# Part of a sliding convolution moved from TensorE to VectorE and GpSimd

## The chip, the cores and the metric

The kernel runs on one core of a Trainium2 chip. The metric is the time of one execution on the device, in microseconds; before the change the median of three runs is 519.91 us (519.69 to 520.58).

TensorE (PE in the profile) multiplies matrices from SBUF into PSUM, which has eight banks here used as four pairs. VectorE (DVE), ScalarE (ACT) and GpSimd (POOL) work element by element; GpSimd's instructions here work in SBUF only. SyncE (SP) issues DMAs. Each engine runs its own instructions in order and waits on semaphores for the others.

## The reference

x is 8 x 3904 x 192; eight heads of 24 channels each have seven taps.

```python
w = softmax(weight, axis=-1)                      # 8 x 7
x_pad = concatenate([zeros((B, 6, D)), x], axis=1)
conv[b, s, h, g] = sum_k w[h, k] * x_pad[b, s + k, h, g]
t = conv.reshape(31232, 192)
out = (((t @ w1) * (t @ w2)) @ w3) @ w_out        # 1024 wide inside, 192 at the end
```

## The kernel before, in words

**Streams and rounds.** The 31,232 tokens are two streams of 15,616 (NS = 2), the first and the last four batches, which are computed side by side. A round is 512 tokens of both streams; there are 31 (the last of 256), in eight groups of four (the last group of three). The product w3 @ w_out is computed once (W_sb), so a round is two products: first_product makes ab = (t w1) * (t w2), TensorE at L381, ScalarE's cast at L389, VectorE's multiply at L400; second_product makes out = ab @ W_sb, TensorE at L434, ScalarE's copy at L439, and an output DMA at L446. In a group the first products of its four rounds come first (the first stage), then the eight second products, two to a round (the second stage).

**Convolution.** TensorE convolves in windows. A window is 64 tokens on 64 partitions, of which 58 come out; a banded 64 x 64 matrix with the taps of a head (Aband) multiplies it. A batch has 68 windows, a stream 272. conv (L274 to L312) takes a block of windows, half of them to the lower and half to the upper 64 output partitions, and convolves nh heads of it: for each head four matmuls (L290) of n x 24 columns, n being half of the block's windows. The result is cast to bf16 into convo (L311). SIZES lists the blocks: six small ones for the start, then six of 36. load_x fetches a block, with a cast to bf16, by DMAs on GpSimd's queue (L119).

**From convolution to product.** The product wants channels on the partitions, the convolution leaves tokens there. So store (L316 on) writes convo to a DRAM tensor, rows, by DMAs on SP's queue (L334), and transposes(R) (L363) reads round R back into xT by three transposing DMAs, also on SP's queue. xT is a ring of four rounds: round R + 4 takes the place of round R, so its transposes wait until round R's first product has read it. send issues the transposes of all rounds that are wholly in rows.

**Order around the change.** The order of each engine's instructions is that of the code. In the loop over groups p (at the end of the kernel), block 6 + p is loaded while the group's first two rounds run (a one-element copy on GpSimd, pace, L592, holds the loads back until the round's product is done) and convolved between the second products: heads 0 to 2 after the second of them, 3 to 5 after the fourth, 6 and 7 after the eighth, and then stored. VectorE casts it, ScalarE one head of it. The convolution is so some six rounds ahead of the products. The output DMAs are issued by SP, in group 0 by GpSimd. Block 5 belongs to group 0 as well. The eight W products (w3_product, L469) precede group 0's second stage.

PSUM pairs are handed out by banks() from a list and given back by drained(); the order of this list decides which earlier reader a matmul waits for.

Of the kernel before, what the change touches and what calls it, by code (L numbers as in the profile page):

```python
# [8 lines left out]
FP32 = mybir.dt.float32  # L9
# [7 lines left out]
def kernel(  # L17
# [34 lines left out]
    FIRST = [sum(SIZES[:b]) for b in range(NB)]  # L52
    PROLOGUE_BLOCKS = 6
    EARLY = SIZES[0] * ST
    MAXN = max(SIZES) // 2

    def tok(i):
        return (i // WB) * S + (i % WB) * ST
# [199 lines left out]
        return p, Aband[:, g, e], bps[:, :, 0:Q]  # L258


    xT = [const.tile([128, RING + Q], BF16, name=f"xT{k}", tag=f"xT{k}") for k in range(NP)]

    convo_of = {}
# [10 lines left out]
    def conv(b, h0, nh, evict=None):  # L274
        n = SIZES[b] // 2
        if h0 == 0:
            convo_of[b] = work.tile([128, n, NP, NS, Q], BF16, tag="convo", bufs=2, name="convo")
        convo = convo_of[b]
        p, cps = banks()
        wd = nh * G  # L280
# [174 lines left out]
    w3T = const.tile([128, JT, DFF], BF16)  # L455
    w3rows = dram.tile([DFF, DFF], BF16, name="w3rows")

    def load_w3(j):
# [100 lines left out]
    P(out=pace, in_=w3T[0:1, JT - 3, DFF - 2:DFF])  # L559
    load_x(5)  # L560
    load_x(6)
    first_product(3)
# [5 lines left out]
    def conv_heads(b, heads, last, f=(nc.vector.tensor_copy,), nh=1):  # L568
        for j, h in enumerate(heads[::nh]):
            conv(b, h, nh, (f[j % len(f)],))  # L570
        if heads[-1] == H - 1:
            first = min(need(sent[0]), FIRST[b] + SIZES[b])
            store(b, last=first)
            send(last)
            store(b, first)
            send(last)

    slots = (range(0, 3), range(3, 6), range(6, H))
    zero(5)
    for jt in range(JT):  # L580
        w3_product(jt)

    groups = [list(range(R, min(R + GROUP, NR))) for R in range(0, NR, GROUP)]
    assert groups[-1][-1] == NR - 1
    for p, rounds in enumerate(groups):
        b = PROLOGUE_BLOCKS + p
        order = rounds[-1:] + rounds[:-1] if rounds[-1] == NR - 1 else rounds
        for j, R in enumerate(order if p else ()):
            first_product(R, behind_conv=j == 0 and b <= NB)
            send(R + GROUP)  # L590
            if j < 2 and b < NB:
                P(out=pace, in_=abT_of[R][0:1, JT - 1, 1, 0:2])  # L592
                load_x(b, (j,))
        if b < NB:
            zero(b)
        ahead = rounds[-1] + GROUP
        at = {1: [(b, slots[0], ahead)], 3: [(b, slots[1], ahead)],
              7: [(b, slots[2], ahead, (V, A))]}
        if p == 0:
            at = {0: [(5, range(0, 6), ahead, (V, A), 2)], 1: [(5, range(6, H), ahead, (V,), 2)],  # L600
                  4: at[1], 5: at[3], 7: at[7]}
# [4 lines left out]
    assert sent[0] == NR  # L606


# [28 lines left out]
```

## Time and profile before

| | us |
|---|---|
| median of 3 runs | 519.91 (519.69 to 520.58) |
| the profiled execution | 520.47 |
| its span, first to last instruction | 518.8 |
| TensorE matmuls busy | 512.4 |
| VectorE busy | 352.8 |
| ScalarE busy | 328.7 |
| GpSimd busy | 58.5 |
| first products, matmuls (L381, all forms) | 319.9 |
| second products, matmuls (L434) | 164.9 |
| convolution, matmuls (L290) | 16.7 |

A row of a group reads: line, engine, operation, output<-input, partitions x elements and type, count | busy us, mean ns of one | idle time of the engine just before, and who ended it. A row of the chain in order of time reads: start, length, what. DMA lines with sixteen engines' share count a packet's time as the profiler saw it.

### The profile page before, as it was taken

The page shows a single profiled execution, that of the slowest core. Times are in us where ns is not written, and L with a number is a line of the kernel's source. Part 1 is how long each engine was busy: PE and PEld are TensorE (multiplying, and loading weights), DVE is VectorE, ACT ScalarE, POOL GpSimd, SP SyncE. Part 2 cuts the span into 40 slices and gives each one's busy share as a digit, 9 for nine tenths or more (in the row PEclk, how much of TensorE's full clock was granted, in tenths as well). Part 3 has the DMA queues.
Part 4 walks back from the last instruction along what each step waited for, and adds up shares of the span by engine and source line. Part 5 has one row for each costly group of instructions (what it writes and reads, how often), then busy time and mean ns, then how long its engine had stood idle before and what let it go on. Part 6 is the DMA issues. An engine that isn't in the chain of part 4 may idle for free.

```text
span 518.8 us, 13029 instructions
## 1 busy us (share of the span) xinstructions
PE 512.4 (99%) x5576; PEld 338.7 (65%) x5576; DVE 352.8 (68%) x334; ACT 328.7 (63%) x415; POOL 58.5 (11%) x98
## 2 busy tenths in 40 slices
PE   8999999999999999999999999999999999999997
PEld 4455797445884558845588455884558845599567
DVE  6778625999439994399943999439994399921980
ACT  6887634777347773477734777347773477734762
POOL 8501522110001200011000120001200000000000
PEclk9999999999999999999999999999999999999999
DMA  9979997599246992469924699246992465124004
GB/s 117 162 145 133 156 201 202 137 178 119 93 134 134 151 121 92 135 117 142 143 92 136 141 141 122 93 136 147 133 121 93 136 146 96 37 92 153 1 3 152
DMA packets 133576, 64.61 MB, mean 125 GB/s; under 512 B 90460, under 2 KB 132798, under 8 KB 133454
## 3 DMA queue, kind: packets, MB, share of 16 engines
q1 hardware_dynamic: 94476, 44.06, 41.7%
q0 software_dynamic: 38896, 19.62, 29.1%
q8 instruction: 43, 0.70, 0.6%
q14 instruction: 15, 0.12, 0.1%
q10 hardware_dynamic: 146, 0.10, 0.1%
HBM read 33.25 MB, written 36.52 MB: 134 GB/s over the span
## 4 chain that ended last, share of the span: by engine, by line
PE 95%; DMA 2%; ACT 2%; DVE 1%; issue 0%; ACTq 0%; DVEq 0%
PE pairs L381 58%; PE pairs L434 31%; PE pairs L290 3%; DMA xT<-rows 2%; DVE abT L400 1%; PE pairs L469 1%; ACT asb L389 1%; PE pairs L206 1%; PE pairs L343 1%; PE pairs L256 0%; ACT wd L186 0%; ACT convo L311 0%; DVE convo L478 0%; ACT xT L355 0%; PE pairs L509 0%
## 5 line engine op out<-in xcount | busy, mean ns | idle before, releaser
L400 DVE TENSOR_TENSOR abT<-asb,pairs 128x1024 bf16<-128x1024 bf16 (+1 forms) x245 | 297.9, 1217 | 52.6 <-ACT asb L389 36.6
L381 PE MATMUL pairs<-xT,wd 64*128 64x512 bf16 (+3 forms) x3000 | 319.9, 371 | 1.1 <-DMA xT<-rows 0.5
L389 ACT CAST asb<-pairs 128x1024 bf16<-128x1024 f32 (+1 forms) x245 | 247.2, 1009 | 66.2 <-PE pairs L381 65.9
L381 PEld LDWEIGHTS <-wd 64*128 64x128 bf16 x3000 | 161.0, 94 | 154.8 <-issue 3.7
L434 PEld LDWEIGHTS <-abT 128*128 128x128 bf16 x1952 | 160.0, 98 | 7.5 <-issue 7.5
L434 PE MATMUL pairs<-W_sb,abT 128*128 128x192 bf16 x1952 | 164.9, 246 | 0.0
L439 ACT COPY osb<-pairs 128x384 f32<-128x384 f32 x122 | 58.3, 478 | 113.8 <-PE pairs L434 113.8
L311 DVE CAST convo<-pairs 128x864 bf16<-128x864 f32 (+5 forms) x58 | 46.4, 854 | 95.8 <-PE pairs L290 74.9
L119 POOL DMA_DIRECT2D xb<-in_x_dram x42 | 32.2, 784 | 3.7 <-PE pairs L381 3.7
L592 POOL COPY pace<-abT 1x2 bf16<-1x2 bf16 x10 | 1.8, 176 | 253.5 <-DVE abT L400 253.5
L290 PE MATMUL pairs<-xb,Aband 64*64 64x432 bf16 (+5 forms) x384 | 16.7, 284 | 0.1
L311 ACT CAST convo<-pairs 128x864 bf16<-128x864 f32 (+4 forms) x20 | 11.8, 626 | 0.4
L290 PEld LDWEIGHTS <-Aband 64*64 64x64 bf16 x384 | 6.9, 106 | 6.8 <-issue 5.7
L446 POOL DMA_DIRECT2D out_dram<-osb x8 | 6.1, 761 | 16.7 <-ACT osb L439 14.1
L439 DVE COPY osb<-pairs 128x192 f32<-128x192 f32 x1 | 0.4, 358 | 11.1 <-PE pairs L434 11.1
L469 PEld LDWEIGHTS <-w3T 128*128 128x128 bf16 x64 | 5.2, 98 | 0.4 <-issue 0.4
L469 PE MATMUL pairs<-wo_b,w3T 128*128 128x192 bf16 x64 | 5.5, 246 | 0.0
L190 POOL COPY wd<-wd 64x768 bf16<-64x768 bf16 x6 | 4.8, 840 | 0.4 <-DMA wd<-in_moe_w_dram 0.4
L206 PE MATMUL pairs<-zeros 128*128 128x512 bf16 x8 | 3.8, 627 | 1.1 <-DVE ones L152 1.1
L343 PE MATMUL pairs<-ident,convo 128*128 128x128 bf16 x48 | 3.9, 219 | 0.7 <-DVE convo L478 0.6
L343 PEld LDWEIGHTS <-convo 128*128 128x128 bf16 x48 | 2.9, 97 | 2.5 <-issue 1.5
L471 ACT CAST W_sb<-pairs 128x192 bf16<-128x192 f32 x8 | 2.6, 320 | 2.8 <-PE pairs L469 2.8
(52 smaller groups left out, 38.8 us busy)
## 6 DMA issues: line engine op xcount, KB each, us to landing
out_dram<-osb SPq DMA_DIRECT2D x52, 384.0 KB
xb<-in_x_dram POOLq DMA_DIRECT2D x16, 432.0 KB, 11.6
rows<-convo SPq DMA_DIRECT2D x5, 648.0 KB
out_dram<-osb POOLq DMA_DIRECT2D x8, 384.0 KB, 3.9
w3rows<-in_moe_w_dram POOLq DMA_DIRECT2D x2, 1024.0 KB, 11.5
xb<-in_x_dram POOLq DMA_DIRECT2D x8, 240.0 KB, 5.5
xT<-rows SPq DMA_TRANSPOSE x81
rows<-convo SPq DMA_DIRECT2D x3, 432.0 KB
```

The source lines that it names most:

```text
L119: nc.gpsimd.dma_start(out=xb[Q * r:Q * r + Q, w:w + m, :], in_=x_spans(r, i, m))
L206: nc.tensor.matmul(t[:, j % 2, :], zeros, zeros[:, 0:1].to_broadcast([128, CH]), start=True, stop=True)
L290: nc.tensor.matmul(view(slice(Q * c, Q * c + Q), r)[:, :, j * G:(j + 1) * G], band_of(h, r), xb[Q * r:Q * r + Q, w0:w0 + n, h * G:(h + 1) ...
L311: f[e % len(f)](out=dst, in_=part)
L343: nc.tensor.transpose(out=tps[:, w, :], in_=convo[:, w, k].rearrange("p r g -> p (r g)"), identity=ident)
L381: nc.tensor.matmul(p[:, r, e * n:e * n + n], wd[i][rs, k, ft * 128:(ft + 1) * 128], xT[k][rs, r0 + c0:r0 + c1], start=(k == 0), stop=(k == ...
L389: nc.scalar.copy(out=asb, in_=pa)
L400: nc.vector.tensor_tensor(out=dst, in0=asb, in1=pb, op=ALU.mult)
L434: nc.tensor.matmul(ops[:, (g - g0) * D:(g - g0) * D + D], ab[:, jt, r, g * 128:(g + 1) * 128], W_sb[:, jt, :], start=(jt == 0), stop=(jt = ...
L439: f(out=osb[:, g0:g0 + per, :].rearrange("p g d -> p (g d)"), in_=ops[:, 0:per * D])
L446: queue.dma_start(out=out[t0:t0 + ng * 128, :].rearrange("(g p) d -> p g d", p=128), in_=osb)
L469: nc.tensor.matmul(wps[:, 0, 0:D], w3T[:, gt, jt * 128:(jt + 1) * 128], wo_b[:, gt, :], start=(gt == 0), stop=(gt == JT - 1))
```

## The change

Blocks. After the start-up blocks 0 to 4 the grid of windows goes on in blocks of 20, 20, 14, 20 and 18 (5 to 9), which end inside round 14. Rounds 16 and 17, 20 and 21, 24 and 25 are each convolved by TensorE as a block of 18 windows of their own (ALONE), in groups 2 to 4. The last 24 windows are the last block, in group 5. Rounds 14 and 15, 18 and 19, 22 and 23, 26 and 27 (SHARED) are not on TensorE: in groups p = 2 to 5 VectorE and GpSimd convolve them.

Shared rounds. load_shared brings 1024 tokens of both streams as 128 partitions of 8 consecutive tokens and the 6 before them, so that a tap is a shift along the free dimension. Where a batch begins inside (7808 in the tile of p = 2, 11712 in that of p = 4), the six rows before it are overwritten with zeros by another DMA, which waits for the load. shared_head convolves one head. GpSimd takes heads 0 to 3: seven multiplications into fp32 tiles, the taps broadcast, and additions, the last of them in two or four pieces into y; all four heads stand at the group's head in its order, and behind them the loads for the next group. VectorE takes heads 4 to 7: ScalarE writes the first tap's product into a PSUM bank, five fused multiply-adds follow there, and the last tap goes in two or four pieces into y. Heads 4 and 5 come before the second stage, 6 after its second and 7 after its fourth product. They use one PSUM pair, held from before the stage to its end. store_shared writes y into rows after the stage, with the transposes of both rounds behind it.

The rest. conv_heads takes two or three heads at a time; ScalarE casts the lone blocks and most of the last one. Taps are computed a second time on all partitions (wv), between the first and the second W product. w3T shares its buffers with the shared tiles. From group 2 on, the transposes of the next group's first two rounds follow the first two first products, with no pace copies.

```diff
-    SIZES = [6, 4, 8, 10, 8, 20] + [36] * 6
-    assert sum(SIZES) == NWIN
+    SIZES = [6, 4, 8, 10, 8, 20, 20, 14, 20, 18]
+    SHARED = {p: ((p + 2) * GROUP - 2, (p + 2) * GROUP) for p in range(2, 6)}
+    ALONE = {p: (p + 2) * GROUP for p in range(2, 5)}
+    CA = 2 * CH
...
+    NA = 2 * (-(-CA // (2 * ST)))
+    GRID = len(SIZES)
+    SIZES += [NA] * len(ALONE) + [24]
...
+    def load_shared(v):
+        t0, W = share(v)
+        xv = work.tile([128, W + PAD, NS, D], BF16, tag="xw", bufs=2, name="xv")
+        for r in range(NS):
+            nc.gpsimd.dma_start(out=xv[:, :, r, :], in_=bass.AP(
+                tensor=x.tensor, offset=(r * TS + t0 - PAD) * D,
+                ap=[[W * D, 128], [D, W + PAD], [1, D]]))
...
+    def shared_head(v, h, f):
...
+        on_vector = f is nc.vector
+        if on_vector:
+            acc = held[0][1][:, h % 2, 0:W * NS * G]
+        else:
+            acc = work.tile([128, W * NS * G], FP32, tag="acc", bufs=2, name="acc")
...
+        if on_vector:
+            nc.scalar.activation(out=flat, in_=xs(PAD), func=ACT.Copy, scale=tap(PAD))
+            for k in range(PAD - 1, 0, -1):
+                f.scalar_tensor_tensor(out=flat, in0=xs(k), scalar=tap(k), in1=flat,
+                                       op0=ALU.mult, op1=ALU.add)
+            for dst, r, cs in parts:
+                f.scalar_tensor_tensor(
+                    out=dst, in0=xv[:, 0:W, r, h * G + cs.start:h * G + cs.stop],
+                    scalar=tap(0), in1=by_row[:, :, r, cs], op0=ALU.mult, op1=ALU.add)
+            return
+        wide = lambda k: tap(k).unsqueeze(2).to_broadcast([128, W * NS, G])
+        f.tensor_tensor(out=flat, in0=xs(PAD), in1=wide(PAD), op=ALU.mult)
+        for k in range(PAD - 1, -1, -1):
+            term = work.tile([128, W * NS * G], FP32, tag="term", bufs=2, name="term")
+            f.tensor_tensor(out=term.rearrange("p (m g) -> p m g", g=G), in0=xs(k),
+                            in1=wide(k), op=ALU.mult)
+            if k:
+                f.tensor_tensor(out=acc, in0=acc, in1=term, op=ALU.add)
+        term = term.rearrange("p (s r g) -> p s r g", r=NS, g=G)
+        for dst, r, cs in parts:
+            f.tensor_tensor(out=dst, in0=by_row[:, :, r, cs], in1=term[:, :, r, cs], op=ALU.add)
...
-    slots = (range(0, 3), range(3, 6), range(6, H))
...
+    at = {
+        (0, 0): [(conv_heads, 5, SHORT, (V, A))],
+        (0, 1): [(conv_heads, 5, LONG), (put_rows, 5, 2 * GROUP - 1), (load_x, 7)],
+        (0, 4): [(conv_heads, 6, SHORT, (V, A))],
+        (0, 5): [(conv_heads, 6, LONG), (put_rows, 6, 2 * GROUP - 1)],
+        (0, 6): [(conv_heads, 7, range(H), (A, V), 3)],
+        (0, 7): [(put_rows, 7, 2 * GROUP - 1)],
+        (1, 1): [(conv_heads, 8, SHORT)],
+        (1, 3): [(conv_heads, 8, LONG), (store, 8),
+                 (conv_heads, 9, range(0, 4))],
+        (1, 7): [(conv_heads, 9, range(4, H), (V, A)), (put_rows, 9, 3 * GROUP - 1)],
+        (5, 0): [(conv_heads, NB - 1, range(0, 2), (A,), 1)],
...
+    for p in ALONE:
+        at[p, 0] = [(conv_heads, GRID - 2 + p, range(0, 4), (A,))]
+        at[p, 3] = [(conv_heads, GRID - 2 + p, range(4, H), (A,)), (store_alone, p)]
+    for p in SHARED:
+        for i, h in ((-1, 4), (-1, 5), (1, 6), (3, 7)):
+            at.setdefault((p, i), []).append((shared_head, p, h, nc.vector))
+    behind = {
+        (1, 0): [(load_x, 8)], (1, 1): [(load_x, 9)], (1, 3): [(load_shared, 2)],
+        (4, 1): [(load_x, NB - 1)]}
...
     for p, rounds in enumerate(groups):
-        b = PROLOGUE_BLOCKS + p
         order = rounds[-1:] + rounds[:-1] if rounds[-1] == NR - 1 else rounds
+        if p in SHARED:
+            for h in range(0, 4):
+                shared_head(p, h, nc.gpsimd)
+            if p + 1 in ALONE:
+                load_alone(p + 1)
+            if p + 1 in SHARED:
+                load_shared(p + 1)
         for j, R in enumerate(order if p else ()):
-            first_product(R, behind_conv=j == 0 and b <= NB)
-            send(R + GROUP)
-            if j < 2 and b < NB:
+            first_product(R, behind_conv=j == 0 and p in (2, 6))
+            if p == 1:
+                send(R + GROUP)
+            elif R + GROUP < NR and (j < 2 or p > 5):
+                transposes(R + GROUP)
+            if p == 1 and j != 2:
                 P(out=pace, in_=abT_of[R][0:1, JT - 1, 1, 0:2])
-                load_x(b, (j,))
...
+            run(behind.get((p, j), ()))
+            if p == 1 and j == 3:
+                load_alone(2)
+        if p in SHARED:
+            held.append(banks())
+            run(at.get((p, -1), ()))
         for i, (R, r) in enumerate((R, r) for R in rounds for r in range(NS)):
             second_product(R, r, R == NR - 1 and r == 1, nc.sync if p else nc.gpsimd)
-            for c in at.get(i, ()) if b < NB else ():
-                conv_heads(*c)
+            run(at.get((p, i), ()))
+        if p in SHARED:
+            drained(held.pop()[0])
+            store_shared(p)
+            for R in range(*SHARED[p]):
+                transposes(R)
```

More of the change, by code (lines that the diff above doesn't have):

```diff
@@ L261, with store_shared @@
+    def store_shared(v):
+        t0, W = share(v)
+        y = shared.pop(v)[1]
+        nc.sync.dma_start(
+            out=rows[t0:t0 + 128 * W, :].rearrange("(p s) c -> p (s c)", s=W),
+            in_=y.rearrange("p s k r q -> p (s k r q)"))
     xT = [const.tile([128, RING + Q], BF16, name=f"xT{k}", tag=f"xT{k}") for k in range(NP)]
@@ L561 @@
     load_x(6)
+    wv = const.tile([128, H, K], FP32)
+    top = const.tile([128, H], FP32)
+    nc.sync.dma_start(out=wv, in_=bass.AP(
+        tensor=weight.tensor, offset=0, ap=[[0, 128], [K, H], [1, K]]))
     first_product(3)
@@ new lines, with run @@
+    for p in ALONE:
+        at[p, 0] = [(conv_heads, GRID - 2 + p, range(0, 4), (A,))]
[6 more added lines that the diff above has]
+        (4, 1): [(load_x, NB - 1)]}
+    def run(calls):
+        for f, *a in calls:
+            f(*a)
@@ L597 @@
[L597 to L601, printed above, removed]
+        if p in SHARED:
[5 more added lines that the diff above has]
+                load_shared(p + 1)
```

96 lines of the change are left out of this document (77 added, 19 removed).

## The prediction

> **What bounds the kernel now.** I read the page first: engine totals, the forty slices, the chain that ended last.
>
> ```profile
> span 518.8 us, 13029 instructions
> PE 512.4 (99%) x5576; PEld 338.7 (65%) x5576; DVE 352.8 (68%) x334; ACT 328.7 (63%) x415; POOL 58.5 (11%) x98
> ...
> DMA  9979997599246992469924699246992465124004
> ...
> PE 95%; DMA 2%; ACT 2%; DVE 1%; issue 0%; ACTq 0%; DVEq 0%
> PE pairs L381 58%; PE pairs L434 31%; PE pairs L290 3%; DMA xT<-rows 2%; DVE abT L400 1%; PE pairs L469 1%; ACT asb L389 1%; PE pairs L206 1%; PE pairs L343 1%; PE pairs L256 0%; ACT wd L186 0%; ACT convo L311 0%; DVE convo L478 0%; ACT xT L355 0%; PE pairs L509 0%
> ```
>
> TensorE is the chain almost everywhere, so an edit pays only in TensorE time. The convolution, L290, has 3% of it. Then the chain in order of time, which prices a group:
>
> ```profile
> 58.94 5.39 PE pairs L469 x64
> ...
> 66.97 0.74 PE pairs L290 x24
> 67.71 2.75 PE pairs L434 x32
> 70.45 0.33 PE pairs L290 x8
> ...
> 88.78 23.17 PE pairs L381 x213
> 111.94 8.86 DMA xT<-rows
> 120.80 0.04 issue
> 120.84 10.11 PE pairs L381 x92
> ...
> 154.22 41.55 PE pairs L381 x384
> 195.77 5.39 PE pairs L434 x64
> 201.16 0.67 PE pairs L290 x12
> 201.83 5.39 PE pairs L434 x64
> 207.21 0.67 PE pairs L290 x12
> 207.88 10.67 PE pairs L434 x128
> 218.55 0.49 PE pairs L290 x8
> 219.04 41.55 PE pairs L381 x384
> ```
>
> A group is 64.82 us (219.04 - 154.22): 41.55 of first products, about 21.4 of second products, and 0.67 + 0.67 + 0.49 = 1.83 for a convolution block of 36 windows. There is no gap. The other engines in group 0's second products and in group 2's two stages (sums by windows; columns PE, PEld, DVE, ACT, POOL, then clock, DMA share, GB/s):
>
> ```profile
> 58.90:88.80 29.90, 29.90 (x388) 27.58 (x388) 11.32 (x15) 11.68 (x27) 7.20 (x11) 1.00 1.07 204
> ...
> 154.20:195.80 41.60, 41.60 (x390) 20.60 (x387) 38.47 (x32) 32.84 (x34) 5.35 (x10) 1.00 0.99 130
> 195.80:219.00 23.20, 23.20 (x290) 21.56 (x291) 7.67 (x11) 7.98 (x17) 0.00 (x0) 1.00 0.36 120
> ```
>
> In the first stage (second row) VectorE is within 8% of TensorE and the DMA engines are full (share 0.99). In the second (third row), VectorE and ScalarE are two thirds idle, the DMA share is 0.36, and GpSimd does nothing. The clock is 1.00 throughout.
>
> **What TensorE loses and keeps.** Convolved windows fall from 272 to 206 (128 + 3 x 18 + 24), because eight rounds leave the grid. A matmul's columns are 12 times the block's windows. Two block sizes have chain rows: 20 windows (240 columns) took 0.74 + 0.33 = 1.07 us, 36 windows (432 columns) 1.83. A line through both gives 0.12 + 0.00396 per column, hence 0.79 for 14 windows (168), 0.98 for 18 (216) and 1.26 for 24 (288). From block 5 on, before: 1.07 + 6 x 1.83 = 12.05. After: three blocks of 20 (3.21), one of 14 (0.79), one of 18 (0.98), three lone blocks of 18 (2.93) and one of 24 (1.26): 9.17. **Saved: 2.9 us.** Bounds: the 216-column block lies between half of 1.83 and the 1.07 of 240 columns, so 0.92 to 1.07, which over four such blocks is -0.2 to +0.4.
>
> Smaller terms. The wait at 111.94, the transposes of round 7, cost group 1 about 0.6 us (130.95 - 88.78 = 42.17 against 41.55). Block 6 is now stored after the sixth second product instead of the eighth, 6 us earlier, but into full DMA engines: 0 to 0.6, I take 0.3 saved. The pair of PSUM banks held for VectorE leaves three pairs in the second stage. A second product's last eviction is 0.48 us (row below) and the narrow convolution slots between two products last 0.3 to 0.6, so the product behind them finds its pair free or about 0.15 us late; some four slots in group 5 and the odd one elsewhere: 0 to 1.0, I take 0.5 lost. The second set of tap weights is some ten tiny instructions on VectorE and ScalarE beside the eight W products (5.4 us of TensorE): 0 to 0.3, taken as nothing.
>
> **VectorE and ScalarE in the second stage.** A tap is a two-input instruction, one input from SBUF and one from PSUM, the operand kinds of L400:
>
> ```profile
> L400 DVE TENSOR_TENSOR abT<-asb,pairs 128x1024 bf16<-128x1024 bf16 x242 | 295.3, 1221 | 51.6 <-ACT asb L389 35.6
> L311 DVE CAST convo<-pairs 128x864 bf16<-128x864 f32 x30 | 30.6, 1054 | 87.8 <-PE pairs L290 67.0 <-DMA out_dram<-osb 20.8
> ...
> L400 DVE TENSOR_TENSOR abT<-asb,pairs 128x696 bf16<-128x696 bf16 x2 | 1.8, 880 | 1.0 <-ACT asb L389 1.0
> ...
> 126.20 6.40 DVE L400 TENSOR_TENSOR abT<-asb,pairs 128x1024 bf16<-128x1024 bf16 x5
> ```
>
> The slope is (1221 - 880) / 328 = 1.04 ns per element, so a tap of 384 elements is 0.56 us, the closing ones of 192, 128 and 64 are 0.36, 0.29 and 0.22. Four heads: 20 x 0.56 + 6 x 0.36 + 2 x 0.29 + 2 x 0.22 = 14.4 us. They replace some 7 us of casts and start when the last product of the stage is done, 1.65 us behind TensorE (in group 1, 126.20 + 6.40 against 130.95): heads 4 and 5 end near 9, 6 near 13, 7 near 16 of 22.4 us. The cover is six microseconds. If a fused multiply-add cost twice the two-input row, 28.8 us would run some 8 past the stage, of which the first stage's slack takes back 2.5 (41.6 - 38.47 less the tail): about 5 us a group, 20 in four.
>
> ```profile
> L439 ACT COPY osb<-pairs 128x384 f32<-128x384 f32 x121 | 58.0, 479 | 112.9 <-PE pairs L434 112.9
> L311 ACT CAST convo<-pairs 128x864 bf16<-128x864 f32 x6 | 5.3, 879 | 0.3
> ...
> L478 ACT CAST convo<-pairs 128x384 bf16<-128x384 f32 x2 | 0.9, 474 | 0.0
> ```
>
> ScalarE gets four first taps (four times 0.47) and the casts of the lone block (four times 0.9 to 1.0): 8.0 + 1.9 + 3.8 = 13.7 of 22.4. A first tap into a bank half waits for the head two before it; head 6's is issued near 6 us and head 4 ends near 5, so the evictions queued behind it on ScalarE aren't held.
>
> **GpSimd, the term that decides.** Per group it gets four heads: 48 instructions of 384 elements and 10 closing ones that make up four times 384, 58 instructions and 19,968 elements. No row shows two inputs there; the nearest:
>
> ```profile
> L119 POOL DMA_DIRECT2D xb<-in_x_dram x42 | 32.2, 784 | 3.7 <-PE pairs L381 3.7
> ...
> L190 POOL COPY wd<-wd 64x768 bf16<-64x768 bf16 x6 | 4.8, 840 | 0.4 <-DMA wd<-in_moe_w_dram 0.4
> ...
> L592 POOL COPY pace<-abT 1x2 bf16<-1x2 bf16 x10 | 1.8, 176 | 253.5 <-DVE abT L400 253.5
> ```
>
> One stream costs (840 - 176) / 766 = 0.87 ns per element over a fixed 0.18. With the copy's rate for two inputs, the floor, a group is 17.3 + 10.2 = 27.5 us; with three times it (two reads and a write in turn), 62.1. I take twice, one stream per input, because the copy is the only streaming row: 34.6 + 10.2 = **44.8 us**.
>
> [...]
>
> What is it late for? Its queue runs heads(p), then the loads of the lone block (four issues of 0.78) and the shared tile of p+1, then heads(p+1), which wait for that tile. The DMA view of 154 to 220 us prices a load (packets, MB, share of 16 engines):
>
> ```profile
> q0 software_dynamic: 4704, 1.77, 24.6%
> ```
>
> 24.6% of 66 us over 4704 packets is 3.45 ns a packet of 384 bytes. The shared tile is 128 x 14 x 2 = 3584 packets, 12.4 us; a lone block 2304, 7.9. The first tile is issued when round 7's product is done, at 132.6 (126.20 + 6.40). The stores of 384 KB that a page row shows to landing bound the new store:
>
> ```profile
> out_dram<-osb POOLq DMA_DIRECT2D x8, 384.0 KB, 3.9
> ```
>
> The tile lands near 146; the zeros of a batch start inside it wait for that (some 3 us), then four issues: heads(2) from 152. Gaps between head sets: 21 us, 24 (with such zeros again) and, with no lone block, 13: 58 together. Groups 2 to 4 are now 41.55 + 21.44 + 0.98 = 64.0 us each, so groups 3, 4, 5 and 6 start at 218.4, 282.3, 346.3 and 410.5 (group 5 keeps 1.26 of convolution). The two shared rounds come third and fourth: first needed 20.8 us into the next group, and before that their store (384 KB landed in 3.9 us; this one is twice that, say 4) and the transposes (8.86 in the chain): GpSimd must end by 8 us into the next group, 418.3 for the last. 152 + 4H + 58 = 418.3 gives **H = 52.1 us**; at 44.8 it ends 29 us early, and beyond 52.1 each microsecond per group is four at the end. At 62.1 that is 40 us. SP issues this store and six transposes behind the last output store and waits there for GpSimd; queued behind are the next group's transposes and outputs, needed a group later.
>
> **Does GpSimd slow VectorE?** In the start-up it copied weights while VectorE multiplied:
>
> ```profile
> 13.76 1.60 POOL L190 COPY wd<-wd 64x768 bf16<-64x768 bf16 x2
> ...
> 14.56 3.75 DVE L400 TENSOR_TENSOR abT<-asb,pairs 128x1024 bf16<-128x1024 bf16 x3 [0.59 <-ACT asb L389]
> ...
> L400 DVE TENSOR_TENSOR abT<-asb,pairs x33: 840/1221/1222, 10.8 to 59.4; 128x1024 bf16<-128x1024 bf16 x30, 128x696 bf16<-128x696 bf16 x2, 128x656 bf16<-128x656 bf16 x1
> ```
>
> The longest multiply there is 1222 ns against a median of 1221, beside copies or not. I cost it at nothing; two-input GpSimd work isn't in the trace, so the other end is a wait of half a GpSimd instruction (0.42 us) for each of the 32 multiplies in a stage, 13.4 less the slack of 2.5, some 11 us in each of four stages.
>
> **The sum.** The profiled execution took 520.47 us (518.8 of it span): -2.9 -0.3 +0.5 = 517.8. The median of the three runs, 519.91, lies 0.56 below that execution, so the forecast for the median is **517.2 us**. About 0.2% (1 us) is what a measurement of this kernel tells from no change.
>
> **Rivals.**
> 1. GpSimd is late (slower). Place: the first product of the third round of groups 3 to 6. It decides from 52.1 us per set of heads. For it: the price rests on a one-input row, and the loads stand between the sets. Against: 7 us of margin in each set. Halfway from the threshold to the upper bound, H = 57, it costs 20 us: 537; all of it spans 519 to 557.
> 2. VectorE becomes the bound, by port waits (4 x 11: 561) or by dear fused taps (537). The multiply rows speak against both.
> 3. The gain is given back: waits of some 3 us, 520. Block 7 is loaded once block 5 has left its buffers (70.78) and convolved after seven second products and two blocks (64.33 + 7 x 2.7 + 2 x 1.07 = 85.4); Its 14 x 128 packets take 6.2 us at 3.45 ns, but the DMA engines are over-full there (share 1.07), and the load waits behind others.
> 4. It does what it says but short matmuls cost more than the line: 518.5; this lies in the forecast's own range.
>
> **Chances.** Forecast with the fourth 0.54 (516.0 to 518.9); GpSimd late 0.29; VectorE 0.09; given back 0.08. Faster by over 0.2%: 0.54 and a hair of the third, 0.55. Within 0.2%: most of the third, 0.07. Slower: 0.38. The range runs from 515.6 (bounds of the savings added, no bank waits) up to 537, where half of the first rival and part of the second are left out.
>
> **What would show it.** Right: L290 in groups 2 to 4 adds to about 1.0 us in the chain, which stays without a transpose wait before the third round; GpSimd's two-input instructions near 0.85 us, a set under 52; L400 still at 1221. Wrong: a DMA or GpSimd piece in the chain some 21 us into groups 3 to 6, growing from group to group (rival 1); multiplies longer than 1222, or taps above 0.6 us (rival 2).

## The result and the profile after

The changed kernel takes 534.82 us (median of 4 runs, 531.53 to 538.59) against 519.88 (519.69 to 520.58): a ratio of 1.027, 95% interval 1.022 to 1.032. It is slower; the forecast was 517.2 with a range up to 537 and a chance of 0.38 for slower. The profiled execution took 534.05 us.

The page of the changed kernel, engine totals, slices and GpSimd's and VectorE's new groups:

```profile
span 532.3 us, 13534 instructions
...
PE 515.2 (97%) x5640; PEld 344.8 (65%) x5640; DVE 385.5 (72%) x423; ACT 348.2 (65%) x459; POOL 254.1 (48%) x333
...
PEclk9999999799999999999999999999899999999999
...
L328 POOL TENSOR_TENSOR acc<-acc,term 128x384 f32<-128x384 f32 x80 | 79.7, 997 | 6.3
L325 POOL TENSOR_TENSOR term<-xv,wv 128x384 f32<-128x384 bf16 x96 | 79.3, 826 | 3.3 <-DMA xv<-zeros 3.3
L314 DVE SCALAR_TENSOR_TENSOR pairs<-xv,wv,pairs 128x384 f32<-128x384 bf16 x80 | 49.8, 622 | 4.2 <-ACT pairs L312 1.9
```

L381 is now L486 (first products), L434 L539 (second), L290 L395 (convolution), L400 L505 (VectorE's multiply), L363 L468 (transposes). TensorE's granted clock dips in two slices (digits 7 and 8). Both lie where it waits for transposes or just behind (who waited for whom: us in total, times, longest):

```profile
PE pairs L486 <- DMA xT<-rows: 9.5, 5, 3.4
PE pairs L539 <- DVE abT L505: 1.7, 4, 0.4
```

And the chain in order of time, where it departs from the one of before:

```profile
82.46 1.90 PE pairs L539 x22
84.36 10.93 DMA xT<-rows
...
95.34 43.83 PE pairs L486 x380
...
162.53 39.62 PE pairs L486 x366
...
202.18 1.02 ACT asb L494
...
203.22 1.23 DVE abT L505
...
204.50 2.80 PE pairs L539 x32
207.30 0.49 PE pairs L395 x16
...
226.98 39.62 PE pairs L486 x366
...
355.87 15.11 PE pairs L486 x139
370.98 10.12 DMA xT<-rows
...
381.14 19.95 PE pairs L486 x170
...
426.50 41.88 PE pairs L486 x384
```

Set side by side, the starts of the groups' first products show where the 13.5 us of span came from (all but 0.2 of it):

| start of group | before | after | lost since the row above |
|---|---|---|---|
| 1 | 88.78 | 95.34 | 6.56 |
| 2 | 154.22 | 162.53 | 1.75 |
| 3, 4, 5 | 219.04, 283.86, 348.68 | 226.98, 291.42, 355.87 | -0.37 each |
| 6 | 413.50 | 426.50 | 5.81 |
| last chain piece | 515.73 | 529.06 | 0.33 |

So groups 2 to 4 do save time, though less than half of what was forecast (0.37 of 64.82 - 64.0), and two places lose it all and more: the turn from group 0 to 1, and group 5. In both TensorE waits for the transposes of a round (5.7 us in three waits, 3.8 in two), and after the wait its granted clock is low. By windows (columns as in the prediction; the last row is group 5, behind its wait):

```profile
88.60:95.30 6.70, 1.06 (x5) 0.22 (x5) 1.27 (x2) 2.45 (x5) 0.75 (x1) 0.90 1.13 168
95.30:100.00 4.70, 4.66 (x23) 1.88 (x24) 1.33 (x2) 2.02 (x2) 0.00 (x0) 0.50 0.95 279
100.00:104.00 4.00, 4.00 (x36) 1.99 (x34) 3.00 (x3) 2.44 (x3) 0.00 (x0) 0.91 0.59 129
...
381.00:385.00 4.00, 3.86 (x24) 1.69 (x25) 1.22 (x1) 1.74 (x2) 1.77 (x3) 0.62 1.41 178
```

At the turn TensorE does 5 matmuls in 6.7 us, then runs at half clock (0.50) for 4.7, doing 23 where it does some 43 at full clock (384 in 41.55 us). That is most of why the chain has 43.83 us where a first stage has 41.55. Ahead of the 0.50 lie 5.7 us of waits in 6.7, ahead of the 0.62 in group 5 the 3.8 us of waits. Behind single waits of 0.4 to 0.5 us the granted clock was 1.00: in the changed kernel in the 4 us behind each of the four for L505 (from 204.5, 268.94, 333.4 and 403.43 us), in the kernel before from 121 to 125 us, behind its wait for round 7.

The DMA engines are full where the first wait builds up (share 1.13, and 1.14 from 71.8 to 84.0 us, where the kernel before has 0.73). What is in the way shows in SP's queue, first before the change, then after:

```profile
77.94 4.18 SPq L363 DMA_TRANSPOSE xT<-rows  x3
```

```profile
79.48 14.64 SPq L468 DMA_TRANSPOSE xT<-rows  x6
```

Before, three transposes took 4.2 us to issue; now six, both rounds' in a row, take 14.6. Beside them, from 71.85 us, runs the load of block 7:

```profile
71.85 2.95 POOL L126 DMA_DIRECT2D xb<-in_x_dram  x4
```

### The profile page after: what moved, and what is told of

Its sections match the earlier page's. It is cut to its first block, busy times and chain, and to the rows that moved or that the text cites. A ratio compares the mean times of both kernels' runs of the same rounds, so it can differ in the third digit from the quotient of the medians.

```text
span 532.3 us, 13534 instructions
## 1 busy us (share of the span) xinstructions
PE 515.2 (97%) x5640; PEld 344.8 (65%) x5640; DVE 385.5 (72%) x423; ACT 348.2 (65%) x459; POOL 254.1 (48%) x333
## 4 chain that ended last, share of the span: by engine, by line
PE 90%; DMA 4%; DVE 3%; ACT 2%; issue 0%; ACTq 0%; DVEq 0%
PE pairs L486 56%; PE pairs L539 30%; DMA xT<-rows 4%; DVE abT L505 2%; PE pairs L395 2%; ACT asb L494 2%; PE pairs L574 1%; PE pairs L448 1%; PE pairs L213 1%; DVE cprod L254 0%; ACT convo L416 0%; DVE convo L583 0%; ACT xT L460 0%; PE pairs L614 0%; PE pairs L263 0%
## 5 line engine op out<-in xcount | busy, mean ns | idle before, releaser
L505 DVE TENSOR_TENSOR abT<-asb,pairs 128x1024 bf16<-128x1024 bf16 (+1 forms) x245 | 298.0, 1217 | 82.5 <-ACT asb L494 53.3
L486 PE MATMUL pairs<-xT,wd 64*128 64x512 bf16 (+3 forms) x3000 | 325.0, 374 | 10.2 <-DMA xT<-rows 9.5
L486 PEld LDWEIGHTS <-wd 64*128 64x128 bf16 x3000 | 165.7, 95 | 163.4 <-issue 16.2
L539 PE MATMUL pairs<-W_sb,abT 128*128 128x192 bf16 x1952 | 165.1, 246 | 1.7 <-DVE abT L505 1.7
L539 PEld LDWEIGHTS <-abT 128*128 128x128 bf16 x1952 | 160.2, 98 | 7.4 <-issue 7.3
L328 POOL TENSOR_TENSOR acc<-acc,term 128x384 f32<-128x384 f32 x80 | 79.7, 997 | 6.3
L325 POOL TENSOR_TENSOR term<-xv,wv 128x384 f32<-128x384 bf16 x96 | 79.3, 826 | 3.3 <-DMA xv<-zeros 3.3
L314 DVE SCALAR_TENSOR_TENSOR pairs<-xv,wv,pairs 128x384 f32<-128x384 bf16 x80 | 49.8, 622 | 4.2 <-ACT pairs L312 1.9
L416 DVE CAST convo<-pairs 128x960 bf16<-128x960 f32 (+7 forms) x22 | 16.6, 803 | 41.3 <-PE pairs L395 35.9
L322 POOL TENSOR_TENSOR acc<-xv,wv 128x384 f32<-128x384 bf16 x16 | 13.3, 830 | 35.9 <-DMA xv<-in_x_dram 35.8
L416 ACT CAST convo<-pairs 128x576 bf16<-128x576 f32 (+11 forms) x47 | 24.8, 594 | 3.5 <-DMA rows<-convo 3.3
L126 POOL DMA_DIRECT2D xb<-in_x_dram x34 | 24.2, 735 | 3.4 <-DMA xb<-in_x_dram 2.4
L331 POOL TENSOR_TENSOR y<-acc,term 128x192 bf16<-128x192 f32 (+2 forms) x40 | 19.3, 508 | 1.3
L395 PE MATMUL pairs<-xb,Aband 64*64 64x216 bf16 (+7 forms) x448 | 13.9, 242 | 0.0
L317 DVE SCALAR_TENSOR_TENSOR y<-xv,wv,pairs 128x192 bf16<-128x192 bf16 (+2 forms) x40 | 12.8, 371 | 0.7
L395 PEld LDWEIGHTS <-Aband 64*64 64x64 bf16 x448 | 8.2, 106 | 5.6 <-issue 5.2
```

The lines of the kernel that those rows point to most:

```text
L126: nc.gpsimd.dma_start(out=xb[Q * r:Q * r + Q, w:w + m, :], in_=x_spans(r, i, m))
L314: f.scalar_tensor_tensor(out=flat, in0=xs(k), scalar=tap(k), in1=flat, op0=ALU.mult, op1=ALU.add)
L325: f.tensor_tensor(out=term.rearrange("p (m g) -> p m g", g=G), in0=xs(k), in1=wide(k), op=ALU.mult)
L328: f.tensor_tensor(out=acc, in0=acc, in1=term, op=ALU.add)
L331: f.tensor_tensor(out=dst, in0=by_row[:, :, r, cs], in1=term[:, :, r, cs], op=ALU.add)
L395: nc.tensor.matmul(view(slice(Q * c, Q * c + Q), r)[:, :, j * G:(j + 1) * G], band_of(h, r), xb[Q * r:Q * r + Q, w0:w0 + n, h * G:(h + 1) ...
```

## The experiments

**Theory:** the change lost three things, none of them on VectorE or GpSimd as engines: block 7's load in front of the transposes of rounds 4 and 5; a wait for the shared rounds' transposes in group 5; and 0.41 us at each turn to the second products, because a PSUM pair is held. **Rivals:** the way block 5 is stored (in one piece, both rounds' transposes behind it) for the first; GpSimd being too slow for the second. All ratios below are to the kernel before, run on the same chip.

**e1_late7: block 7 moved out of group 0.**

```diff
-        (0, 6): [(conv_heads, 7, range(H), (A, V), 3)],
-        (0, 7): [(put_rows, 7, 2 * GROUP - 1)],
+        (1, 0): [(conv_heads, 7, range(H), (A, V), 3), (put_rows, 7, 2 * GROUP)],
-        (0, 1): [..., (put_rows, 5, 2 * GROUP - 1), (load_x, 7)],
+        (0, 1): [..., (put_rows, 5, 2 * GROUP - 1)],
-        (1, 0): [(load_x, 8)], (1, 1): [(load_x, 9)], ...
+        (1, 0): [(load_x, 7), (load_x, 8)], (1, 1): [(load_x, 9)], ...
```

> The changed kernel with block 7's load and convolution moved from group 0 (load behind the second second product, at 72 us) to group 1 (load behind its first first product, convolution behind its first second product); one buffer more for loads, the same matmuls. Theory (this load fills the DMA engines while rounds 4 and 5 are stored and transposed): group 1's first product starts near 89 us instead of 95.3, and its first stage takes 41.6 to 42.2 us instead of 43.8, because TensorE's clock does not drop; 8 us less, about 526.5. Rival (block 5 stored in one piece, with both rounds' transposes behind it on SP's queue, makes round 4 late): nothing moves, 533 to 536, and group 1 still starts behind 94 us.

Measured: 532.02 us (1.0216, 1.0171 to 1.0261). Its chain:

```profile
82.74 5.39 PE pairs L539 x64
88.13 41.55 PE pairs L486 x384
```

Group 1 starts at 88.13 with no wait and full clock, although block 5 is stored as in the changed kernel and its six transposes stand in a row (10.77 us to issue instead of 14.64): that way of storing does not make the turn late by itself. The time fell by some 3 us instead of 8 because the edit made a new wait: round 9's transposes, left to the end of group 1, stood behind round 10's and 11's stores, and TensorE waited 6.5 us in group 2.

**e5_spare: the same load added to the kernel before.**

```diff
+    spare = const.tile([128, 14, D], BF16)
...
             for c in at.get(i, ()) if b < NB else ():
                 conv_heads(*c)
+            if p == 0 and i == 1:
+                load_spare(0)
+                load_spare(1)
```

Nothing reads the tile, so this kernel does all of its work and one load more. (e1_late7 took block 7's convolution and store out of group 0 as well as its load; here the load stands alone.)

> The kernel before, with a load of the size of block 7's (four DMAs of 168 KB into a tile that nothing reads) put on GpSimd's queue behind the second second product of group 0. Theory: it does there what block 7's load did, the transposes of round 4 land late, group 1 starts some 4 to 7 us late and its clock drops: 525 to 528. Rival (the way block 5 is stored): the time stays within 0.5 us of 519.9.

Measured: 528.05 us (1.0113, 1.0049 to 1.0176). Four DMAs, 0.69 MB of 65, cost some 6 us by the ratio. The chain of the profiled execution:

```profile
60.74 5.39 PE pairs L469 x64
...
84.16 7.28 DMA xT<-rows
...
91.47 24.32 PE pairs L381 x223
115.79 10.75 DMA xT<-rows
...
126.58 13.14 PE pairs L381 x94
...
162.99 41.55 PE pairs L381 x384
```

Group 2 starts 8.8 us later than in the kernel before (162.99 against 154.22). Of that, 1.8 us come before the load is issued (the W products start at 60.74 instead of 58.94); the other 7.0 come behind it. But they are not where the theory had them: the turn to group 1 loses only 0.9 us of them, with a wait of 0.4, and the long wait, 4.1 us, comes ahead of group 1's fourth round. Behind it 94 matmuls take 13.14 us (10.2 at the rate of 384 in 41.55), and the page's slice of 118.7 to 131.9 us has the granted clock at digit 7. The kernel before had little room there: its own chain has 8.86 us of transposes ahead of that round, and a wait of 0.5.

So a load of this size at this place is expensive in either kernel. The 6.6 us at the turn need more than one thing, though: block 5 stored in one piece loses nothing there without block 7 (e1_late7), and the load loses 0.9 there where block 5 is stored in two pieces. The changed kernel has both, and block 7's convolution and store besides; no run takes these apart.

**e3_pair: another pair held.**

```diff
+            free[0], free[1] = free[1], free[0]
             held.append(banks())
```

> The changed kernel with the second free PSUM pair held for VectorE instead of the first. Theory (the 0.41 us before the first second product of groups 2 to 5 is the wait for a pair that VectorE's last but one multiply drains, as the pair that ScalarE's cast had drained earlier was the one held): these four waits go, 1.7 us in all, about 533, which three rounds may not tell; the trace decides. Rival (the first second product waits for the data of the multiply): the waits stay at 0.41.

Measured: 533.61 us (1.0264, 1.0191 to 1.0337), too near to tell by time (the waits for transposes were 1.5 us longer in its profiled execution, 11.0 against 9.5). The trace tells it: the four waits for L505 are gone, and the turn is back to what it was.

```profile
224.13 41.55 PE pairs L486 x384
265.68 2.75 PE pairs L539 x32
268.42 0.49 PE pairs L395 x16
```

The pair that ScalarE's cast drains first had been given to VectorE, which doesn't need it until it has done the last multiply itself.

**e2_ahead: loads of the next group ahead of the heads.**

```diff
         if p in SHARED:
+            if p + 1 in SHARED:
+                load_shared(p + 1)
+            if p + 1 in ALONE:
+                load_alone(p + 1)
             for h in range(0, 4):
                 shared_head(p, h, nc.gpsimd)
-            if p + 1 in ALONE:
-                load_alone(p + 1)
             if p + 1 in SHARED:
-                load_shared(p + 1)
+                pad_shared(p + 1)
...
```

Here pad_shared is the zeros for a batch start, split off from load_shared.

> The changed kernel with the loads of the next group's shared tile and lone block issued on GpSimd's queue ahead of the group's four heads instead of behind them (the zeros for a batch start stay behind). Theory (GpSimd is late in group 5 because its queue stands idle 18 to 29 us for each load): its sets of heads follow each other with gaps under 2 us, the fourth head of group 4 ends well before group 5 starts, no wait for transposes in group 5, first stage there 42 us instead of 47.6: about 5.6 less, 529. Rival (the transposes of the shared rounds are late by themselves, through full DMA engines): group 5 keeps a wait of 3 to 4 us before its third round, 533 to 536.

Measured: 535.34 us (1.028, 1.0234 to 1.0326): nothing gained, where 529 was expected. Group 5's wait is gone (its first stage has no wait for transposes), as the theory said, but one of 3.6 us, nearly as long, stands in group 2, where these loads, issued at 159 and 161 us, meet the transposes of rounds 10 and 11 (DMA share 1.29 from 161 to 175 us):

```profile
161.37 13.60 PE pairs L490 x125
174.97 11.44 DMA xT<-rows
...
186.45 21.05 PE pairs L490 x170
```

The store of the shared rounds shows the same without a wait: GpSimd is done at 217 us, SP issues the store at 233.34, and the transposes behind it can go only at 245.04, 11.7 us later, with the loads for group 4 (228.39) beside it and a DMA share of 1.19 from 228 to 245 us.

**e7_mid: loads between the third and fourth head.**

```diff
-            for h in range(0, 4):
+            for h in range(0, 3):
                 shared_head(p, h, nc.gpsimd)
+            if p + 1 in SHARED:
+                load_shared(p + 1)
             if p + 1 in ALONE:
                 load_alone(p + 1)
+            shared_head(p, 3, nc.gpsimd)
             if p + 1 in SHARED:
-                load_shared(p + 1)
+                pad_shared(p + 1)
...
```

> The changed kernel with the next group's loads issued between GpSimd's third and fourth head, so that they end in the quiet part of a group, neither at a stage's turn nor between the sets of heads. Theory (a load that coincides with the store and the transposes of the shared rounds makes them late, as in e2_ahead, where GpSimd was done 16 us before its result was stored and TensorE still waited 1.8 us for the transposes in group 3): no wait for transposes in groups 3 to 6, group 5's first stage 42 us, about 529. Rival (GpSimd's own work is too long for a group): its sets end later from group to group and a wait in group 5 or 6 stays.

(The wait named there as group 3's was group 2's; in group 3 of e2_ahead the transposes came just in time.) Measured: 528.65 us (1.0159, 1.0116 to 1.0203). The profiled execution is the shortest of the four, 522.4, with only 3 us lost at the start of group 1. From group 2 on there is no wait for transposes in the trace: the rival, GpSimd's work too long for a group, is out. The edit does two things at once, however. It takes the loads away from the store, and it lets the sets of heads follow each other with gaps of 0.3 to 4.5 us, so that group 4's set ends at 324.14, 25.7 us ahead of group 5 (349.79); this run does not tell which of the two was needed.

**e9_five: only group 5's loads moved, with group 4's heads meant to keep their time.**

```diff
+            if p == 4:
+                load_shared(5)
+                load_x(NB - 1)
+                pad_shared(4)
             for h in range(0, 4):
                 shared_head(p, h, nc.gpsimd)
...
```

> The changed kernel with only the loads for group 5 (its shared tile and the last block) moved: from behind group 4's heads on GpSimd's queue to ahead of them, right behind the loads for group 4, so that GpSimd's heads of group 4 keep their time. Theory (the store and the transposes of group 4's shared rounds run into these two loads): GpSimd still ends some 8 to 10 us into group 5, but the transposes land within 13 us of that, and TensorE's wait in group 5 falls from 3.8 us to under 1. Rival (GpSimd is simply too late): the wait stays at 3 to 5 us. The start of group 1 and the four waits of 0.41 us stay as they are, so 528 to 531 by the theory, 533 to 536 by the rival.

Measured: 544.49 us (1.0422, 1.0362 to 1.0481). This missed its purpose: the zeros for the batch start, 4.5 KB that group 4's heads wait for, went into the queue behind the moved loads and took 14.42 us, so that the set of heads ended at 381.8 instead of 364.9, and TensorE waited 13.3 us. It is a clean look at GpSimd being late, though, with no load beside the store:

```profile
380.70 1.14 POOL y L335 x2
...
390.51 21.05 PE pairs L490 x170
```

From the end of the heads to TensorE's next round are 8.7 us (390.51 - 381.84). In the changed kernel, with the loads for group 5 issued by GpSimd right behind its last head (364.79), the same way took 16.3 (381.14 - 364.85). SP's queue shows which part of it grew, first in this run, then in the changed kernel:

```profile
381.86 0.35 SPq L365 DMA_DIRECT2D rows<-y  x1
385.22 15.49 SPq L472 DMA_TRANSPOSE xT<-rows  x12
```

```profile
364.87 0.35 SPq L361 DMA_DIRECT2D rows<-y  x1
368.33 22.13 SPq L468 DMA_TRANSPOSE xT<-rows  x12
```

The transposes wait for the store, and the store took about as long in both (3.4 and 3.5 us). From the transposes' first issue to TensorE's round it is 5.3 us here (390.51 - 385.22) and 12.8 there (381.14 - 368.33): in group 5 the loads held up the transposes.

**e6_late7b, e8_all, e8b_all, e10_actq, e11_alone2: putting it together.** e6_late7b is e1_late7 with rounds 8 and 9 sent together; e8_all adds e7_mid's and e3_pair's edits.

> As e1_late7, with the transposes of round 9 sent together with round 8's right after block 7 (in e1_late7 they were left to the end of group 1, where nine transposes stood in front of round 9's product). Theory: the start of group 1 stays as in e1_late7 (88 us, no clock drop), the wait of 6.5 us in group 2 goes; what is left of the three waits is group 5's: 521 to 526. Rival (block 5's way of storing): already fallen by e1_late7; the other rival here is that a wait moves to group 2 again because block 7 is convolved too late for round 8.

> e6_late7b, e7_mid and e3_pair together: block 7 in group 1, loads between the third and fourth head, the second free pair held. Theory (three waits and the clock's drop behind two of them are all that the change lost; its saving of TensorE time is 2.9 us as predicted): 517 to 518, with convolution of 0.49 + 0.49 us in the chain of groups 2 to 4 and nothing else new: 0.4 to 0.6 percent under the kernel before. Rival (the work on VectorE and GpSimd slows the products): above 520.

Measured: 530.82 (1.018, 1.0123 to 1.0237) and 525.41 (1.0078, 1.0052 to 1.0105), both above what was expected. Neither has a wait for transposes left, but both have a new one of 6.2 and 5.1 us at the start of group 2, for ScalarE without an output tile: on SP's queue six transposes wait for block 7's store and hold up the output stores (in e8_all the store is issued at 134.27 us, the transposes at 142.98, the next output stores at 152.74). e6_late7b also keeps the four waits for the pair.

e6_late7b tells something about group 5 too. It leaves the loads for group 5 right behind group 4's heads, as in the changed kernel, and still TensorE does not wait there: the set of heads ends at 356.04, 1.2 us into group 5 (which starts at 354.85), instead of 9.0. Ending earlier is enough, then, with the loads beside the transposes.

e8b_all sends round 9's transposes four second products later than round 8's (the diff is against e8_all):

```diff
-        (1, 0): [(conv_heads, 7, range(H), (A, V), 3), (put_rows, 7, 3 * GROUP - 1)],
+        (1, 0): [(conv_heads, 7, range(H), (A, V), 3), (put_rows, 7, 2 * GROUP)],
+        (1, 5): [(send, 2 * GROUP + 1)],
```

> As e8_all, with round 8's transposes alone behind block 7 and round 9's four second products later. In e8_all six transposes in a row waited on SP's queue for block 7's store; the output stores stood behind them, ScalarE ran out of output tiles, and TensorE waited 5.1 us at the start of group 2. Theory: without this wait and the clock's drop behind it, 522.7 less 5.1 and 1.8 of span, so about 517.5 as the time on a chip that gives 520 before: 0.3 to 0.6 percent under the kernel before. Rival (another queue takes the wait over): 519 or above, and the trace names it.

Measured: 523.28 (1.0033, 1.0001 to 1.0065), where about 517.5 was expected. 3.2 us of the wait are left. Then the output stores of group 1 on ScalarE's queue (e10_actq), and the first lone block's load put off into group 2 as well (e11_alone2):

```diff
-            second_product(R, r, R == NR - 1 and r == 1, nc.sync if p else nc.gpsimd)
+            second_product(R, r, R == NR - 1 and r == 1,
+                           (nc.gpsimd, nc.scalar)[p] if p < 2 else nc.sync)
...
                 shared_head(p, h, nc.gpsimd)
+                if (p, h) == (2, 1):
+                    load_alone(2)
...
             if p == 1 and j == 3:
-                load_alone(2)
```

> As e8b_all, with the output stores of group 1 issued by ScalarE instead of SP, so that they no longer stand behind block 7's to 9's stores and transposes. Theory: TensorE's last wait, 3.2 us at the start of group 2 for ScalarE without an output tile, and the clock's drop behind it (43.34 instead of 41.55 us) go, 5 us less: a span near 516.4, 517.5 to 518.5 as a time, 0.3 to 0.5 percent under the kernel before. Rival (the output stores themselves land too late, beside the loads): the wait stays above 2 us.

> As e10_actq, with the load of the first lone block put off from the end of group 1's first stage to between GpSimd's second and third head of group 2, which takes 2304 packets out of group 1's second stage. Theory (if the wait of e8b_all is one for DMA engines): whatever e10_actq leaves of it goes, 517.5 to 518.5. If e10_actq has no wait left, this run equals it within 0.5 us, and varies less.

Measured: e10_actq 526.23 (1.0096, 1.0063 to 1.0129), a miss: the wait took other forms, 2.6 us for transposes and 1.1 for ScalarE, in or just behind a second stage of group 1 with a DMA share of 1.04. e11_alone2 521.04 (0.9986, 0.9955 to 1.0016): the same as the kernel before, above the 517.5 to 518.5 expected, but with no wait for transposes left. All that it changes in e10_actq is the place of one load. With the load moved, three transposes on SP's queue take 5.85 us to issue (from 152.97) instead of 9.98 (from 155.61), though the DMA share from 130 to 155 us is no lower (1.07).

**e12_early2: the first shared tile loaded one round earlier still, and the later loads back behind the heads.**

```diff
-        ..., (1, 3): [(load_shared, 2)],
+        ..., (1, 2): [(load_shared, 2)],
...
-            for h in range(0, 3):
+            for h in range(0, 4):
                 shared_head(p, h, nc.gpsimd)
-                if (p, h) == (2, 1):
+                if (p, h) == (2, 2):
                     load_alone(2)
...
-            shared_head(p, 3, nc.gpsimd)
```

> As e11_alone2, but the first shared tile is loaded behind the third first product of group 1 instead of the fourth, so that it lands before group 1's second stage and GpSimd's first set of heads starts some 20 us earlier; the later loads stand behind the heads again (shared tile first), and the first lone block behind the third head. Theory (e11_alone2's loss of 1.7 us around the turn from group 1 to group 2 comes from a DMA share above 1 in group 1's second stage): group 2 takes 64.0 us as groups 3 and 4 do, the set of heads ends some 15 to 30 us before its group does, no wait for transposes anywhere: a span near 517, 518 to 519.5 as a time, up to 0.3 percent under the kernel before. Rival (loads and transposes cannot all be placed in these groups): a wait of 1 to 5 us appears in group 1 or 2, 520 to 525.

Measured: 518.50 us, lowest 518.34, against 521.15, lowest 519.69, of the kernel before in the same runs: 0.9943, 0.9908 to 0.9979. This version is faster than the changed kernel and, by half a per cent or less, than the kernel before: the lowest times differ by 1.35 us (0.26%), and the ratio says more only because the kernel before scatters further upward in these runs. Its chain:

```profile
87.95 41.55 PE pairs L490 x384
...
218.01 41.55 PE pairs L490 x384
259.56 2.75 PE pairs L543 x32
262.30 0.49 PE pairs L399 x16
262.80 8.03 PE pairs L543 x96
270.82 0.49 PE pairs L399 x16
271.32 10.67 PE pairs L543 x128
281.98 41.55 PE pairs L490 x384
```

A group takes 63.97 us (281.98 - 218.01), TensorE waits for no transpose anywhere, and the chain's last piece starts at 513.08, 2.65 us before the one of before. The loads for groups 3 to 5 stand behind the heads as in the changed kernel; what differs is that group 4's set ends at 325.41, 20.5 us ahead of group 5 (345.96).

## Why the prediction was wrong, point by point

**TensorE's saving: right as a sum, once nothing waits.** The lone blocks take 0.49 + 0.49 us as forecast (0.98), and a group without the pair's wait 63.97 (64.0). From block 5 on the convolution takes 9.19 us in e12_early2 (1.07 + 1.07 + 2.63 + 2.94 + 1.48; forecast 9.17), though the last block took 1.48 instead of 1.26 and the middle ones less. e12_early2's chain ends 2.65 us earlier where the sum had 2.7 (2.9 + 0.3 - 0.5), and that nearness is partly luck: the wait for round 7 gave 0.6 instead of 0.3, the pair's 0.5 was not lost, and the first products of groups 2 and 6 took 41.89 and 41.88 us instead of 41.55. Less of it reaches the time: the span is 2.1 us shorter (516.7 against 518.8), the lowest time 1.35.

**VectorE and ScalarE: right.** A tap is 0.62 us (0.56 forecast, 1.12 the upper bound), ScalarE's first tap 0.59 (0.47), and GpSimd does not slow VectorE's multiplies. In group 3's first stage of the changed kernel, with GpSimd busy for 26 of 42 us, the multiplies (min, median, max) are

```profile
L505 DVE TENSOR_TENSOR abT<-asb,pairs x31: 1220/1221/1223, 228.8 to 267.7; 128x1024 bf16<-128x1024 bf16 x31
```

The kernel before has 1220/1221/1222 in group 2's first stage, with GpSimd busy for 5.35 of 41.6 us. The wait of 0.42 us a multiply that the prediction set as the other end, and that rival 2 calls port waits, was the author's estimate; no multiply shows it. The marks that the prediction set for rival 2, multiplies above 1222 ns or taps above 0.6 us, were drawn too fine: 1223 and 622 ns are past them, and VectorE is no bound.

**GpSimd's own work: size off.** A set of heads took 48.6 to 51.3 us (the first 49.4, 163.34 to 212.71; two of the four include a wait for zeros) against 44.8 taken and 52.1 as the threshold. For the two without it (48.6), the rows' estimate, twice the copy's rate, was low by 3.8 us. A multiplication with a broadcast tap takes 0.83 us, an addition of two fp32 tiles 1.00. No set reached the threshold, but the error used up margin, as the point on rival 1 shows.

**The step that failed: a load was priced for itself alone.** The prediction counted how long each load takes and asked whether its reader waits. For block 7 it found 6.2 us against some 14 and gave the rest a rival of "some 3 us" with a chance of 0.08. But block 7 was there in time; what waited were the store and transposes of rounds 4 and 5, issued from the same moment on (SP's queue begins the store at 71.92 us, GpSimd's the load at 71.85). That cost 6.6 us, and 1.8 more in group 1, mostly the clock at half speed (0.50 for 4.7 us), a price that no term had (the sum took the clock as 1.00 throughout). With block 7 out of group 0 the loss is gone (e1_late7); the same load alone costs the kernel before 7 us, most of it ahead of a later round (e5_spare). The load is a cause, then; why it strikes at the turn here and a round later there stays open (block 5 stored in one piece is one difference).

**The same step in rival 1, with GpSimd's size beside it.** The prediction had group 4's set end 14.9 us ahead of group 5 (152 + 3 x 44.8 + 21 + 24 = 331.4 against 346.3); it ended 9.0 us into it (364.85 against 355.87), 1 past the limit of 8. Of these 23.9 us, 14.9 are the three sets (149.3 us instead of 134.4), 7.2 the gaps for the loads (29.2 and 23.0 instead of 21 and 24), 3.2 the later start (0.8 us behind group 2's start instead of 2.4 ahead), less 1.4 for groups that took longer than 64.0. The limit itself was set with 13 us for store and transposes, from rows of a kernel in which no load stood beside them; the way is 8.7 us alone and 16.3 beside the loads that GpSimd issues as soon as its heads are done. So TensorE lost 5.8 us. With 8.7 us for the way the set would have been in time (9.0 + 8.7 against 20.8), and so it would with the sets at 44.8 (16.3 - 5.9); both are arithmetic from two runs, and no run took only this load away with GpSimd's end unchanged, as e9_five was meant to. Rival 1 named the place and the direction. GpSimd was late, but its rate does not make it so by itself: e7_mid and e6_late7b have the same instructions on it and no such wait.

**The held pair: wrong place.** It was priced at the convolution slots, 0.5 us in all; the loss was at the turn from first to second products, 0.41 x 4 = 1.7 us, and one swap in the list takes it away (e3_pair).

**Smaller.** The wait for round 7 in group 1 (0.6) did go in e1_late7 and all that follow from it, whose group 1 has 41.55 us. The range's lower end, 515.6, does not come out of the terms that it is said to add up (519.91 - 3.1 - 0.6 = 516.2); nothing hangs on it.

## What to carry to other kernels

A load whose own reader had time was expensive here all the same: alone it cost the kernel before 7.0 us (e5_spare), and in the changed kernel it was under way with the store that TensorE's transposes waited for, at a DMA share of 1.14 where the kernel before has 0.73. So look in the slices for where the DMA engines are full, and at what the chain waits for behind them. The price of taking work off the bound engine was here in the moved transfers and the queue order, and repairs put the wait elsewhere (5.1 us for an output tile in e8_all, 2.6 for transposes in e10_actq), so follow TensorE's waits after each edit. TensorE, 97% busy in the changed kernel, paid twice for waits of several microseconds, once for the wait and once for the clock after it (5.7 us, then 0.50 for 4.7; 3.8 us, then 0.62 for 4). And an engine off the critical path has a deadline of its own: add up its work, its gaps and the way behind it together, since here no part alone used up the margin and the sum did.

## What the runs showed of the hardware that had not been expected

The store of 768 KB took 3.4 us with no loads beside it (e9_five: 381.86 to 385.22 on SP's queue), 3.5 where the loads were issued at the same moment (the changed kernel, 364.87 to 368.33), and 8.5 to 13.0 where they were already on their way (the changed kernel, 292.44 to 300.93 and 229.03 to 242.07; e2_ahead 11.7). A DMA of 4.5 KB took 14.42 us behind larger ones on GpSimd's queue (e9_five). The kernel before scatters from 519.69 to over 527 us in its 17 runs on one chip, while the 12 of e12_early2 there stay within 518.34 to 523.17; whether the waits of group 1, which e5_spare shows to be near, cause that was not looked into.
